# Redrawn tables for the order of a two-MLP kernel, and its last output piece issued by SyncE

## The chip, the cores and the metric

The kernel runs on one core of a Trainium2 chip. The metric is device time in microseconds (us), the median over runs of the same program; the profile is one further execution. The engines are named as in the profile: PE is TensorE (matrix products), DVE is VectorE, ACT is ScalarE, POOL is GpSimd, and SP is SyncE, which here only issues DMAs.

## The reference

Attention over 32 memory slots, then a GELU-like MLP, then an RMS norm and a gated MLP. All arrays are fp32; there are 4 x 576 = 2304 tokens of width 512.

```python
a = exp(phi - max(phi, axis=2))                     # phi: (4, 8, 576, 32)
a = a / (sum(a, axis=2) + 1e-9)
k_m = einsum('bhsm,bhsd->bhmd', a, k)               # q, k, v: (4, 8, 576, 64)
v_m = einsum('bhsm,bhsd->bhmd', a, v)
attn = softmax(q @ k_m.T / sqrt(64))                # over the 32 slots
x = (attn @ v_m).transpose(0, 2, 1, 3).reshape(2304, 512)
h = x @ w_in                                        # 512 -> 2048
x = (h * sigmoid(1.702 * h)) @ w_out                # 2048 -> 512
xn = x / sqrt(mean(x * x, axis=-1) + 1e-6) * rms_g
out = (silu(xn @ w_gate) * (xn @ w_val)) @ w_out2   # 512 -> 1536 -> 512
```

## The kernel before

**Tiles and stages.** The batch is worked in two pairs `pr` of 2 x 576 = 1152 tokens. Attention runs per unit `(b, g)`: batch b, four heads g. `att_k1t` to `att_k5` make the softmax over phi (maxima through a transpose, exponentials, sums) and the small memory keys and values, `att_q1` to `att_q4` the softmax of the queries, which ends in `attnT`. The memory values are multiplied into the first weight (`vm_part`), so that the first MLP is `a_g1` (tokens by vm, then the GELU form, `gf`, split into `gr`) and `a_g2` (by w_out, added into `x2`). `norm_1` to `norm_4` are the RMS norm: squares and their sums, column sums on PE (tile `pnm`), a reciprocal root r by Newton steps on DVE, and its transposes back on PE (`pnr`). `t_a` to `t_d` make the operands of the second MLP, whose gate and value products `s_g3` forms from seven products by the A, S and T blocks of a Strassen-like scheme (tiles `ps_A...`, `ps_S...`), and `s_g4` multiplies by the last weight and adds into `oacc`. `put` writes `oacc` out in pieces of rows; for the last tile of 128 tokens `s_end` works in two halves of 256 columns.

**Precision.** Each fp32 operand is split into a high part that PE multiplies at full rate and the low rest, and each product is three products. For weights this is `w_conv`: two ACT operations on the raw bits, a clamp (`tensor_scalar` with max and min, which the code gives to DVE), two DVE operations on bits, a copy of the high part on ACT and a subtraction of the low part. For weights of the first MLP the clamp works in tile `pad`, for those of the second in tile `cv`; the split weights are written to a cache in DRAM (`cache_a`, `cache_b`, `cache_s`) for the second pair. `w_load` is the DMA of the raw weights (`raw_...`).

**What sets the order.** No instruction is issued where its code stands. The functions add operations to a `Plan`; at the end `Plan.issue` gives all of them to the engines in the order of `Plan.order`. That is a list scheduler with a cost for every operation (`Plan.cost`): on each engine it takes, of the operations that can start soonest, the one with the earliest due time. Due times come from `Plan.dues`: the order of the code on PE, carried back through what depends on what. Two tables bend this. `HASTE` takes a step by its name and arguments (`"att_q4 1 0 0"`) and moves its due time earlier by so many microseconds, and by that what it depends on. `OTHER` names single operations of a step by their place in it; `Plan.add` puts them on DVE if the code gave them to POOL and the other way round:

```python
if k in self.OTHER.get(self.step, ()):
    op.eng = "POOL" if op.eng == "DVE" else "DVE"
```

DMAs all lie on the queue of SP, in planned order, with one exception: in `put`, the smaller row pieces of the last column half are issued by ACT. Where the plan leaves PE idle before a tile, `Plan.fill` puts in products of a constant (`ones_r`). Since `Plan.issue` hands out everything, nearly all rows of the trace have its line (587 before, 611 after).

Of the kernel before, what the change touches and what calls it, by code (L numbers as in the profile page):

```python
# [117 lines left out]
class Plan:  # L118
# [12 lines left out]
    UNIT = {"cache_a": 131072, "cache_b": 65536, "cache_s": 131072}  # L131

    HASTE = {
        "a_g2 0 0 3": 146.2,
        "a_g2 1 1 0": 118.8,
        "att_k1t 0 0": 235.5,
        "att_k2 3 1": 107.7,
        "att_q1 2 1 1": 44.9,
        "att_q3 2 0 0": 108.0,
        "att_q4 1 0 0": 162.7,  # L140
        "att_q4 3 0 0": 115.0,
        "ld_src 0 0 2": 228.6,
        "norm_3 0 2": 113.0,
        "norm_4 0 0 2": 124.5,
        "norm_4 1 1 1": 120.2,
        "s_g4 1 2 1": 212.8,
        "s_g4 1 5 6 False": 27.0,
        "vm_part 0 1 1 0": 174.7,
        "vm_part 1 6 1": 114.4,
        "w_conv c 2 val 0": 124.3,  # L150
        "w_load a 0 1 in 0": 395.9,
    }

    OTHER = {
# [114 lines left out]
    }  # L269

    def __init__(self, nc):
# [18 lines left out]
    def add(self, op):  # L290
        k = self.count[self.step] = self.count.get(self.step, -1) + 1
        op.step = self.step
        if k in self.OTHER.get(self.step, ()):
            op.eng = "POOL" if op.eng == "DVE" else "DVE"
# [296 lines left out]
def kernel(  # L591
# [51 lines left out]
    V, G, A, PE, SP = plan.DVE, plan.POOL, plan.ACT, plan.PE, plan.SP  # L643
# [801 lines left out]
    def put(pr, kk, cols=slice(0, None), last=False):  # L1445
        parts = []
        n0 = kk * P
        while n0 < kk * P + P:
            bb, r = divmod(n0, S)
            r0 = n0 - kk * P  # L1450
            if 2 * pr + bb < N9:
                ln = R9
                to = out_9[2 * pr + bb, r // R9]
            else:
                par, r = divmod(r, HALF)
                cc, p0 = divmod(r, CP)
                ln = min(CP - p0, kk * P + P - n0)
                to = out_v[2 * pr + bb, 2 * cc + par, p0 : p0 + ln]
            parts.append((ln, to[:, cols], oacc[pr][r0 : r0 + ln, kk, cols]))
            n0 += ln  # L1460
        parts.sort(key=lambda x: -x[0])
        for i, (ln, to, x) in enumerate(parts):
            (A if last and i else SP).dma_start(out=to, in_=x)

# [203 lines left out]
    for j, (*key, t) in enumerate(slots):  # L1668
        i = groups.index(tuple(key))
# [39 lines left out]
    for j, (*key, t) in enumerate(slots):  # L1709
        key = tuple(key)  # L1710
        i = groups.index(key)
# [91 lines left out]
```

## Time and profile before

| | us |
|---|---|
| three runs | 837.25, 839.19, 841.02 (median 839.19) |
| profiled execution, its time | 839.06 |
| its span, from first to last instruction | 836.8 |
| PE busy | 819.9 |
| DVE busy | 595.2 |
| ACT busy | 475.7 |
| POOL busy | 246.5 |

The mean granted clock of PE is 0.998 of full speed. Busy times are over the whole span; a wait of PE is read from the view that lists what PE waited for, and from the timelines around it, in which a row shows the start, the duration, the engine, what is written from what, and in brackets the idle time of the engine before it and who ended it.

### The profile page before, as it was taken

The numbers are of one execution on the slowest core, as the hardware profiler recorded it, in microseconds if no ns is written. First come the engines' busy times: TensorE is split into PE (matmuls) and PEld (weight loads), VectorE is DVE, ScalarE is ACT, GpSimd is POOL, SyncE is SP. The second block draws the span as 40 slices with busy tenths as digits, with TensorE's granted clock in tenths as the row PEclk, the third lists the DMA queues.
The fourth block names the chain that finished last, engine by engine and source line by source line (L and its number), as shares of the span: only waits on it lengthen the run. The fifth ranks groups of instructions, "written<-read, shape, count | busy, mean of one in ns | idle before, by whom it ended". The sixth has DMA issues, their size and how long they took to land.

```text
span 836.8 us, 15237 instructions
## 1 busy us (share of the span) xinstructions
PE 819.9 (98%) x5893; PEld 784.1 (94%) x5893; DVE 595.2 (71%) x955; ACT 475.7 (57%) x822; POOL 246.5 (29%) x198
## 2 busy tenths in 40 slices
PE   9899999999999999999999999999999999999997
PEld 7689999999999999999999999999999999999996
DVE  5869599798797778989788688667595334544445
ACT  6897978788788567656666545335352332222221
POOL 3472854475353443345721411001010000000000
PEclk9999999999999999999999999999999999999999
DMA  9995666957967678654666569363356452632504
GB/s 346 297 271 134 225 220 199 298 168 258 281 219 242 223 253 281 231 189 152 180 204 221 176 230 343 129 230 153 112 194 190 157 177 73 205 129 98 176 1 113
DMA packets 76918, 166.92 MB, mean 199 GB/s; under 512 B 7344, under 2 KB 29616, under 8 KB 76848
## 3 DMA queue, kind: packets, MB, share of 16 engines
q1 hardware_dynamic: 76800, 165.93, 60.5%
q8 instruction: 46, 0.75, 0.4%
q14 instruction: 24, 0.20, 0.1%
q10 hardware_dynamic: 48, 0.03, 0.0%
HBM read 106.69 MB, written 59.24 MB: 198 GB/s over the span
## 4 chain that ended last, share of the span: by engine, by line
PE 77%; DMA 6%; ACT 5%; DVE 5%; POOL 3%; issue 2%; SPq 0%; DVEq 0%; POOLq 0%; ACTq 0%
PE pg L587 41%; PE ps_A L587 22%; PE ps_S L587 9%; DMA raw_a_in<-in_moe_w_in_dram 2%; PE pvm L587 2%; DMA cache_b<-cv 2%; DMA stage<-in_v_dram 1%; PE pk L587 1%; PE pq L587 1%; POOL gr L587 1%; POOL pad L587 1%; DVE pad L587 1%; ACT gf L587 1%; DMA kmisc<-in_phi_dram 1%; ACT gr L587 1%
## 5 line engine op out<-in xcount | busy, mean ns | idle before, releaser
L587 PE MATMUL pg<-gr,a_outh 128*128 128x384 f32 (+1 forms) x736 | 193.2, 334 | 2.0 <-DVE x L587 1.3
L587 PEld LDWEIGHTS pg<-gr,a_outh 128*128 128x128 f32 x736 | 132.6, 188 | 2.7 <-DVE x L587 1.6
L587 PE MATMUL pg<-gr,a_outl 128*128 128x384 f32 (+1 forms) x368 | 121.9, 331 | 0.0
L587 ACT COPY c<-ps_A 128x576 f32<-128x576 f32 x72 | 46.1, 640 | 126.1 <-PE ps_A L587 124.9
L587 PE MATMUL pg<-s_o,pp 128*128 128x512 f32 (+1 forms) x438 | 112.2, 387 | 0.0
L587 POOL TENSOR_TENSOR gr<-gf,gr 128x576 fp32r<-128x576 f32 (+2 forms) x62 | 73.1, 1192 | 101.3 <-ACT gr L587 87.6
L587 DVE TENSOR_TENSOR x<-x,pg 128x768 f32<-128x768 f32 (+1 forms) x86 | 79.4, 928 | 26.8 <-PE pg L587 20.0
L587 PEld LDWEIGHTS pg<-s_o,pp 128*128 128x128 f32 x438 | 80.0, 188 | 14.8
L587 DVE TENSOR_TENSOR oacc<-oacc,pg 128x1024 f32<-128x1024 f32 (+2 forms) x55 | 56.5, 1026 | 44.8 <-PE pg L587 44.3
L587 PE MATMUL ps_A<-tba,s_A 128*128 128x288 f32 x576 | 83.4, 295 | 0.0
L587 DVE TENSOR_TENSOR c<-c,ps_S 128x576 f32<-128x576 f32 x48 | 36.2, 754 | 60.8 <-PE ps_S L587 44.7
L587 PEld LDWEIGHTS ps_A<-tba,s_A 128*128 128x128 f32 x576 | 79.0, 188 | 0.4
L587 PEld LDWEIGHTS pg<-gr,a_outl 128*128 128x128 f32 x368 | 69.2, 188 | 0.0
L587 ACT ACTIVATE gf<-pg 128x576 f32<-128x576 f32 x64 | 41.3, 649 | 36.1 <-PE pg L587 29.3
L587 PE MATMUL pg<-s_o,tbd 128*128 128x512 f32 x216 | 60.9, 390 | 0.0
L587 DVE TENSOR_TENSOR c<-c 128x576 f32<-128x576 f32 x44 | 34.0, 772 | 25.0 <-ACT c L587 24.0
L587 ACT CAST gr<-gf 128x576 fp32r<-128x576 f32 (+2 forms) x92 | 45.9, 528 | 2.1 <-PE pg L587 0.5
L587 PEld LDWEIGHTS pg<-s_o,tbd 128*128 128x128 f32 x216 | 39.6, 188 | 7.3
L587 PE MATMUL ps_S<-tbb,s_S 128*128 128x288 f32 x288 | 42.2, 295 | 0.0
L587 PE MATMUL ps_A<-tbc,s_S 128*128 128x288 f32 x288 | 42.1, 295 | 0.0
L587 PE MATMUL ps_S<-tbc,s_S 128*128 128x288 f32 x288 | 42.0, 295 | 0.0
L587 PE MATMUL ps_A<-tbb,s_S 128*128 128x288 f32 x288 | 42.0, 295 | 0.0
(248 smaller groups left out, 1786.1 us busy)
## 6 DMA issues: line engine op xcount, KB each, us to landing
cache_s<-s_S SPq DMA_DIRECT2D x24, 512.0 KB, 4.4
s_S<-cache_s SPq DMA_DIRECT2D x24, 512.0 KB, 4.1
cache_b<-cv SPq DMA_DIRECT2D x36, 256.0 KB, 4.6
raw_a_in<-in_moe_w_in_dram SPq DMA_DIRECT2D x16, 512.0 KB, 5.1
raw_a_out<-in_moe_w_out_dram SPq DMA_DIRECT2D x16, 512.0 KB, 5.8
raw_c_gate<-in_moe_w_gate_dram SPq DMA_DIRECT2D x12, 512.0 KB, 5.2
raw_c_val<-in_moe_w_val_dram SPq DMA_DIRECT2D x12, 512.0 KB, 4.9
raw_c_o<-in_moe_w_out_dram SPq DMA_DIRECT2D x12, 512.0 KB, 4.4
```

The source lines that it names most:

```text
L587: getattr(self.real[op.eng], op.name)(*op.args, **op.kw)
```

## The change

Both tables are replaced. `HASTE` goes from 18 entries to 27, and some of the new ones are negative, so that a step falls due later. `OTHER` is drawn anew; among others, the clamps of `pad` that lie on POOL go from 17 to 6, those of `cv` from 14 to 20. In `put` the condition goes: all pieces are issued by SP. What is computed stays the same, as do the tiles, the loads and the matrix products.

```diff
     HASTE = {
-        "a_g2 0 0 3": 146.2,
...
+        "att_q4 1 0 0": 212.3,
...
+        "s_end 1 5 8": -74.9,
...
     OTHER = {
...
-        "w_conv b 7 vg": (1,),
+        "w_conv b 9 vg": (0, 2, 5),
+        "w_conv c 0 gate 0": (2,),
...
@@ def put
         parts.sort(key=lambda x: -x[0])
         for i, (ln, to, x) in enumerate(parts):
-            (A if last and i else SP).dma_start(out=to, in_=x)
+            SP.dma_start(out=to, in_=x)
```

The first place is the head, where the loads of the first two units and of the first weights share the queue of SP. `stage0_1` holds k, v and q of unit (0, 1), `kmisc2_0` phi of unit (2, 0), `raw_a_0_1_in_1` half of a raw weight, and `cache_a` receives the split weights of the group before. Before, on SP:

```order
L587 DMA raw_a_0_0_out_1_160<-in_moe_w_out_dram 128x1024
L587 DMA raw_a_0_1_in_0_172<-in_moe_w_in_dram 128x2x512
L587 DMA stage0_1_118<-in_q_dram 128x2x576
L587 DMA cache_a_98<-a_0_0_inh_122 128x1024
L587 DMA raw_a_0_1_in_1_174<-in_moe_w_in_dram 128x2x512
L587 DMA kmisc2_0_239<-in_phi_dram 96x2x192 x2
L587 DMA cache_a_98<-a_0_0_inl_123 128x1024
```

After, on SP:

```order
L611 DMA stage0_1_118<-in_v_dram 128x2x576
L611 DMA raw_a_0_1_in_0_172<-in_moe_w_in_dram 128x2x512
L611 DMA stage0_1_118<-in_q_dram 128x2x576
L611 DMA kmisc2_0_239<-in_phi_dram 96x2x192
L611 DMA raw_a_0_1_in_1_174<-in_moe_w_in_dram 128x2x512
L611 DMA kmisc2_0_239<-in_phi_dram 96x2x192
L611 DMA cache_a_98<-a_0_0_inh_122 128x1024
L611 DMA cache_a_98<-a_0_0_inl_123 128x1024
```

Both writes to `cache_a` now stand behind the raw weight `raw_a_0_1_in_1` and behind the two loads of phi; the last half of the weight before, `raw_a_0_0_out_1`, has moved ahead of the load of v. Earlier in the queue, q of unit (0, 0) has moved ahead of phi of that unit.

On ACT, a little later in the head: `pad` and `raw_a_...` are the first two operations of `w_conv`, `stage0_1` (384 and 192 wide) the exponentials of the query softmax of unit (0, 1), `vm0_0h` the high part of the first `vm_part`, `attnT0` the result of `att_q4`. Before:

```order
L587 ACTIVATE pad_121<-raw_a_0_1_out_1_179 128x512
L587 ACTIVATE raw_a_0_1_out_1_179<-raw_a_0_1_out_1_179,ulp_97 128x512
L587 ACTIVATE stage0_1_118<-stage0_1_118 128x384
L587 CAST vm0_0h_161<-pvm_164 64x256 x2
L587 ACTIVATE pad_121<-raw_a_0_2_in_0_234 128x512
L587 ACTIVATE stage0_1_118<-stage0_1_118 128x192
L587 CAST attnT0_139<-pq4_140 128x384
```

After:

```order
L611 ACTIVATE stage0_1_118<-stage0_1_118 128x384
L611 CAST vm0_0h_161<-pvm_163 64x256 x2
L611 ACTIVATE stage0_1_118<-stage0_1_118 128x192
L611 CAST vm0_0h_161<-pvm_164 64x256 x2
L611 CAST attnT0_139<-pq4_140 128x384
L611 ACTIVATE pad_121<-raw_a_0_2_in_0_234 128x512
L611 ACTIVATE raw_a_0_2_in_0_234<-raw_a_0_2_in_0_234,ulp_97 128x512
```

The exponential of 192 columns and the copies of `vm0_0h` have gone ahead of the conversion of `raw_a_0_2_in_0`, and that conversion behind the first copy into `attnT0`. Earlier in ACT's order, both operations of the conversion of `raw_a_0_1_in_1` now stand ahead of the copy of `pk5` (the memory keys of unit (0, 0)); before, only the first did.

On POOL, in the same stretch, clamps of `pad` stood between the small operations of the softmax; they are on DVE now. Near the addition into `x2_0` from `pg2_306` (at 112 us in the trace of before), two subtractions of `a_0_3_outl` that POOL had are on DVE, ahead of that addition.

The second place is the norm of the second pair's first tile, on PE. `pnm` are the column sums, `pnr` the transposes of r, and the products between them belong to the gated MLP of the first pair. Before:

```order
L587 MATMUL pnm_798<-ones_f_91,sm_797 128x1 x3
L587 MATMUL ps_A12_812<-tba0_661,s0_1_A11_788 128x288 x12
L587 MATMUL ps_A11_784<-tbd0_779,s0_0_A22_753 128x288 x12
L587 MATMUL ps_A11_811<-tbb0_674,s0_1_S1_789 128x288 x12
L587 MATMUL pnr_805<-ident_90,r_799 128x128 x3
```

After:

```order
L611 MATMUL pnm_798<-ones_f_91,sm_797 128x1 x3
L611 MATMUL ps_S1_800<-tbc0_690,s0_0_S3_754 128x288 x12
L611 MATMUL ps_A11_784<-tbd0_779,s0_0_A22_753 128x288 x12
L611 MATMUL ps_A11_811<-tba0_661,s0_1_A11_788 128x288 x12
L611 MATMUL ps_A12_812<-tba0_661,s0_1_A11_788 128x288 x12
L611 MATMUL pnr_805<-ident_90,r_799 128x128 x3
```

Four products of twelve matmuls stand between column sums and transposes in place of three. The column sums of another norm (`pnm_566`, at 276 us in the trace of before) have moved later in PE's order by some 44 us of products.

The third place is the end of SP's order, the output pieces of the last tile. Before, the last piece of 32 rows was issued by ACT:

```order
L587 DMA out_0_dram<-oacc1_1065 64x512 x2
L587 DMA out_0_dram<-oacc1_1065 96x256
L587 DMA out_0_dram<-oacc1_1065 32x256
L587 DMA out_0_dram<-oacc1_1065 96x256
L1798 UNCONDITIONAL_BRANCH
```

After:

```order
L611 DMA out_0_dram<-oacc1_1065 64x512 x2
L611 DMA out_0_dram<-oacc1_1065 96x256
L611 DMA out_0_dram<-oacc1_1065 32x256
L611 DMA out_0_dram<-oacc1_1065 96x256
L611 DMA out_0_dram<-oacc1_1065 32x256
L1822 UNCONDITIONAL_BRANCH
```

The piece now stands last on SP, and ACT issues no DMA any more.

## Rows read from the trace of the kernel before

**Rows 1.** The page, busy us with share of the span and number of instructions.

```profile
PE 819.9 (98%) x5893; PEld 784.1 (94%) x5893; DVE 595.2 (71%) x955; ACT 475.7 (57%) x822; POOL 246.5 (29%) x198
```

**Rows 2.** Timelines of PE, ACT and SP at the tail: start us, us, engine, operation.

```profile
831.29 1.00 PE L587 MATMUL pg<-s_o,pp 128*128 128x256 f32 x7
...
832.78 0.43 ACTq L587 DMA_DIRECT2D out_dram<-oacc  x1
...
833.92 0.42 SPq L587 DMA_DIRECT2D out_dram<-oacc  x1
```

**Rows 3.** What PE waited for, whole span: us in total, times, longest us.

```profile
PE pq L587 <- ACT stage L587: 1.4, 1, 1.4
PE pnr L587 <- DVE r L587: 1.4, 1, 1.4
PE pg L587 <- DVE x L587: 1.3, 1, 1.3
...
PE pq L587 <- DVE stage L587: 1.2, 2, 0.7
PE pk L587 <- DVE mx L587: 1.1, 2, 0.6
PE pq L587 <- POOL stage L587: 0.9, 2, 0.6
...
PE pnm L587 <- ACT gf L587: 0.6, 1, 0.6
```

**Rows 4.** Timeline of all engines, 424 to 434 us.

```profile
427.77 1.75 PE L587 MATMUL ps_A<-tbb,s_S 128*128 128x288 f32 x12
...
428.70 1.44 POOL L587 TENSOR_TENSOR c<-c 128x576 f32<-128x576 f32 x1 [4.95 <-ACT c L587]
428.78 1.38 DVE L587 SCALAR_TENSOR_TENSOR r<-r 128x3 f32<-128x3 f32 x1
...
430.90 0.51 PE L587 MATMUL pnr<-ident,r 128*128 128x128 f32 x3 [1.37 <-DVE r L587]
```

**Rows 5.** Windows: us, busy of PE, PEld, DVE, ACT, POOL, clock, DMA share, GB/s.

```profile
8.00:10.00 2.00, 2.00 (x10) 1.74 (x10) 1.53 (x5) 1.97 (x4) 0.00 (x0) 1.00 1.05 386
340.00:400.00 60.00, 59.87 (x389) 59.54 (x387) 56.78 (x73) 36.49 (x61) 24.30 (x17) 1.00 0.59 201
440.00:832.00 392.00, 392.00 (x2503) 366.30 (x2502) 231.43 (x353) 146.22 (x250) 28.51 (x23) 1.00 0.48 164
```

**Rows 6.** Timeline of ACT in the head.

```profile
24.77 0.66 ACT L587 ACTIVATE pad<-raw_a_in 128x512 f32<-128x512 f32 x1 [1.33 <-DMA raw_a_in<-in_moe_w_in_dram]
...
25.74 0.80 ACT L587 ACTIVATE raw_a_in<-raw_a_in,ulp 128x512 uint32<-128x512 uint16 x1
...
35.45 0.67 ACT L587 ACTIVATE pad<-raw_a_in 128x512 f32<-128x512 f32 x1 [0.61 <-DMA raw_a_in<-in_moe_w_in_dram]
36.02 0.35 ACT L587 ACTIVATE stage<-stage 128x192 f32<-128x192 f32 x1
```

**Rows 7.** Timeline of POOL in the head.

```profile
33.10 1.92 POOL L587 TENSOR_SCALAR pad<-pad 128x512 f32<-128x512 f32 x1 [0.43 <-ACT pad L587]
35.09 0.25 POOL L587 TENSOR_SCALAR stage<-stage 128x6 f32<-128x6 f32 x1
```

**Rows 8.** Timeline of all engines, 106 to 118 us.

```profile
108.89 2.37 DVE L587 SCALAR_TENSOR_TENSOR pad<-raw_a_out,pad 128x512 uint32<-128x512 uint32 x1
...
110.10 1.92 POOL L587 TENSOR_SCALAR pad<-pad 128x512 f32<-128x512 f32 x1
...
111.18 0.68 DVE L587 SCALAR_TENSOR_TENSOR pad<-pad,raw_a_in 128x512 uint32<-128x512 uint32 x1
...
113.65 0.45 PE L587 MATMUL pg<-gr,a_outh 128*128 128x384 f32 x1 [1.35 <-DVE x L587]
```

**Rows 9.** Clamps by line and form: count, busy us, mean ns, idle us before.

```profile
L587 POOL TENSOR_SCALAR pad<-pad 128x512 f32<-128x512 f32 x17 | 35.6, 2095 | 19.4 <-ACT pad L587 19.3
L587 DVE TENSOR_SCALAR pad<-pad 128x512 f32<-128x512 f32 x15 | 7.2, 493 | 3.8 <-ACT pad L587 3.6
```

More of the change, by code (lines that the diff above doesn't have):

```diff
@@ L133 @@
     HASTE = {
-        "a_g2 0 0 3": 146.2,
[L135 to L149, printed above, removed]
@@ L150 @@
-        "w_conv c 2 val 0": 124.3,
-        "w_load a 0 1 in 0": 395.9,
+        "a_g1 0 0 1": 159.8,
+        "att_k3 2 0": 106.1,
+        "att_k3s 3 1": 130.1,
+        "att_k5 2 1": 88.9,
+        "att_q1 2 1 1": 83.8,
+        "att_q3s 1 1 0": 174.7,
+        "att_q4 1 0 0": 212.3,
+        "att_q4 2 1 0": 83.8,
+        "ld_src 0 0 2": 389.2,
+        "norm_1 1 2": 132.5,
+        "norm_3 0 1": 100.0,
+        "norm_4 0 0 0": 121.1,
+        "norm_4 0 2 0": 121.1,
+        "s_end 1 5 8": -74.9,
@@ L152 @@
+        "s_g3 1 9 2": 80.1,
+        "s_g4 1 0 0": 95.9,
+        "s_g4 1 4 4": 60.3,
+        "s_g4 1 5 3 False": 21.4,
+        "s_g4 1 5 5 False": -141.8,
+        "s_g4 1 5 7 False": -40.0,
+        "t_d 0 0": 194.3,
+        "vm_part 0 1 1 0": 219.3,
+        "vm_part 1 6 1": 117.0,
+        "w_conv a 0 2 in 1": 83.7,
+        "w_load a 0 1 in 0": 427.4,
+        "w_load c 5 gate 1": 131.2,
+        "w_load s 1 vg": 184.9,
     }
     OTHER = {
+        "a_g1 0 0 1": (14,),
         "a_g1 0 0 2": (14,),
[4 rows of a table removed]
+        "a_g1 0 1 3": (14,),
@@ L160 @@
+        "a_g1 0 2 0": (14,),
         "a_g1 0 3 1": (14,),
         "a_g1 0 3 3": (14,),
[3 rows of a table removed]
+        "a_g1 0 4 0": (14,),
+        "a_g1 0 4 1": (16,),
+        "a_g1 0 4 2": (14,),
+        "a_g1 0 4 3": (14,),
+        "a_g1 0 5 1": (16,),
+        "a_g1 0 5 3": (14,),
         "a_g1 0 6 0": (14,),
+        "a_g1 0 6 1": (16,),
+        "a_g1 0 6 3": (14,),
         "a_g1 1 0 0": (14,),
[16 rows of a table removed]
+        "a_g1 1 0 3": (14,),
+        "a_g1 1 2 1": (14, 16),
+        "a_g1 1 2 3": (14,),
+        "a_g1 1 3 2": (14, 16),
@@ L183 @@
+        "a_g1 1 3 3": (14,),
+        "a_g1 1 4 0": (14,),
+        "a_g1 1 4 1": (16,),
+        "a_g1 1 5 1": (14, 16),
+        "a_g1 1 5 2": (14, 16),
+        "a_g1 1 5 3": (14,),
+        "a_g1 1 6 1": (14,),
+        "a_g1 1 6 2": (14, 16),
+        "a_g1 1 6 3": (14,),
+        "a_g1 1 7 1": (14,),
+        "a_g1 1 7 2": (14,),
+        "a_g1 1 7 3": (14,),
         "att_k3 1 0": (2,),
@@ L185 @@
         "att_k3 2 1": (2,),
[6 rows of a table removed]
+        "att_k3s 0 0": (0,),
+        "att_k3s 0 1": (0,),
+        "att_k3s 1 0": (0, 1),
+        "att_k3s 1 1": (0,),
+        "att_k3s 2 0": (2,),
+        "att_k3s 2 1": (0,),
+        "att_k3s 3 0": (1,),
+        "att_k3s 3 1": (2,),
         "att_k4 0 0": (23,),
[1 row of a table removed]
         "att_k4 1 1": (27,),
[9 rows of a table removed]
+        "att_k4 3 0": (27,),
+        "att_q3s 0 0 0": (1,),
+        "att_q3s 0 1 0": (1, 3),
+        "att_q3s 0 1 1": (3,),
+        "att_q3s 1 0 0": (1,),
+        "att_q3s 1 1 0": (1,),
+        "att_q3s 2 0 0": (1,),
+        "att_q3s 2 1 0": (3,),
+        "att_q3s 3 0 0": (1,),
+        "att_q3s 3 1 0": (3,),
+        "norm_1 0 0": (2, 3),
+        "norm_1 0 2": (3,),
+        "norm_1 1 0": (2, 3),
         "norm_1 1 1": (2, 3),
[3 rows of a table removed]
+        "norm_1 1 2": (2,),
+        "norm_2 0 1": (12,),
+        "norm_2 1 1": (9,),
         "norm_2 1 2": (12,),
[15 rows of a table removed]
+        "s_g3 0 0 2": (26, 28, 29),
+        "s_g3 0 1 2": (29, 33),
+        "s_g3 0 11 2": (28, 30),
+        "s_g3 0 2 2": (26,),
+        "s_g3 0 7 2": (26, 33),
+        "s_g3 1 3 2": (31,),
+        "s_g3 1 6 2": (26, 28),
+        "s_g3 1 7 2": (26,),
+        "t_a 0 0": (3,),
+        "t_b 0 0": (1, 3),
+        "t_b 0 1": (0, 1, 3),
+        "t_c 0 0": (1, 4),
+        "t_c 0 1": (1, 2, 7),
+        "t_c 1 0": (5,),
+        "t_c 1 1": (2, 5),
+        "t_d 0 1": (1,),
         "w_conv a 0 0 in 0": (6,),
@@ L227 @@
         "w_conv a 0 1 in 0": (6,),
[4 rows of a table removed]
+        "w_conv a 0 1 in 1": (6,),
+        "w_conv a 0 2 in 1": (6,),
+        "w_conv a 0 2 out 0": (2,),
         "w_conv a 0 3 in 1": (2,),
[20 rows of a table removed]
+        "w_conv a 0 3 out 0": (6,),
+        "w_conv a 0 3 out 1": (6,),
+        "w_conv a 0 4 in 0": (2,),
+        "w_conv a 0 4 in 1": (2, 6),
+        "w_conv a 0 4 out 0": (6,),
+        "w_conv a 0 4 out 1": (6,),
+        "w_conv a 0 5 out 1": (6,),
+        "w_conv a 0 6 in 1": (2,),
+        "w_conv a 0 7 in 0": (2,),
+        "w_conv a 0 7 in 1": (6,),
+        "w_conv a 0 7 out 0": (6,),
+        "w_conv b 0 vg": (2, 5),
+        "w_conv b 1 vg": (11,),
+        "w_conv b 10 o2": (1,),
+        "w_conv b 10 vg": (2,),
+        "w_conv b 11 vg": (1, 2),
+        "w_conv b 2 vg": (11, 14),
+        "w_conv b 3 vg": (0, 1, 2, 3, 5, 11, 14),
+        "w_conv b 4 vg": (1, 5, 8),
+        "w_conv b 5 vg": (1,),
         "w_conv b 6 vg": (11,),
[1 row of a table removed]
+        "w_conv b 9 vg": (0, 2, 5),
+        "w_conv c 0 gate 0": (2,),
+        "w_conv c 0 gate 1": (2,),
         "w_conv c 0 val 1": (2,),
[2 rows of a table removed]
         "w_conv c 1 o2 0": (2,),
+        "w_conv c 2 gate 0": (2,),
         "w_conv c 2 gate 1": (2,),
[1 row of a table removed]
+        "w_conv c 2 o2 0": (2,),
         "w_conv c 2 val 1": (2,),
@@ L263 @@
         "w_conv c 3 o2 1": (2,),
+        "w_conv c 3 val 0": (2,),
+        "w_conv c 4 gate 0": (2,),
         "w_conv c 4 gate 1": (2,),
[1 row of a table removed]
+        "w_conv c 4 o2 0": (2,),
+        "w_conv c 4 val 0": (2,),
         "w_conv c 5 gate 0": (2,),
[1 row of a table removed]
+        "w_conv c 5 gate 1": (2,),
+        "w_conv c 5 o2 0": (2,),
         "w_conv c 5 val 0": (2,),
+        "w_conv c 5 val 1": (2,),
     }
```

83 rows, old and new, of the table OTHER are left out of this document.

## Prediction

> **What bounds the kernel now.** I read the profile from the outside in. The busy table says that TensorE (PE) is busy for 819.9 of 836.8 us [rows 1]: the span is PE's own work with 16.9 us of gaps, and no other engine is near a bound over the whole. The change leaves every matrix product and every load as it is and draws only their order and the engine of some small operations anew. So it can take from these 16.9 us and add to them, and nothing else. Part of the gaps is the tail, in which the last results leave the chip. The tail is read from the queues: ScalarE issues its piece at 832.78 and SyncE its last one at 833.92, and the span ends at 836.8 [rows 2]; the last matmuls start at 831.29 and last 1.00 us, so the tail is 836.8 − 832.3 = 4.5 us. There remain 16.9 − 4.5 = 12.4 us, the start and the waits inside the program. The table of what PE waited for lists them; seven of its fourteen rows carry the argument, from 1.4 us down to 0.6 [rows 3]. The last of them by time is at 430.90 [rows 4]; from 440 to 832 us PE is busy without a gap [rows 5], so there the change has nothing to win, only to lose.
>
> The timelines around the largest waits say who is late, and it is never an engine's total. In the head ScalarE stands 1.33 us before a conversion whose raw weights have not landed, and the copy that PE wants is queued behind that conversion [rows 6]. A little later an exponential at 36.02 stands behind another such conversion, which idled 0.61 us for its DMA [rows 6], and a small GpSimd (POOL) operation at 35.09 behind a clamp of 1.92 us [rows 7]. Near 112 us VectorE (DVE) is late with an addition: one of its operations took 2.37 us beside a POOL clamp of 1.92, where the same operation took 0.68 next to it [rows 8]. Near 430 one step of the reciprocal root r took 1.38 us for three numbers per partition, beside a POOL addition of 1.44 [rows 4].
>
> **The change part by part.** The sum is made against the profiled run, 839.06 us with a span of 836.8; the median of the three runs lies 0.13 us higher, which I neglect.
>
> *Head, loads.* The 512 KB of raw weights now come ahead of a 512 KB write to the cache in the queue. In the first stretch of rows 5 the transfers run at 386 GB/s, in the two later ones at 201 and 164; at 386, 512 KB take 1.36 us, about the 1.33 that ScalarE idled. In exchange one more conversion of 0.80 us [rows 6] stands ahead of the copy. I take 1.33 − 0.80 = 0.55 us off PE's 1.4 [rows 3]; bounds are the whole 1.4, and nothing, if the load comes no sooner. The queries q now stand before phi; 576 KB at 386 GB/s is 1.5 us by which the softmax over phi starts later. PE spends those first 16 us partly on dummy products, which absorb it: I take +0.3, from 0 to +1.5.
>
> *Head, softmax of the first two units.* The exponential no longer stands behind the conversion that waits for its DMA, and no POOL clamp of 1.92 us stands ahead of the small POOL operations. The waits of PE for this chain are 1.2 (DVE) and 0.9 (POOL) [rows 3], 2.1 in all. A released chain usually meets its next link, here DVE, which has taken over the clamps at 0.49 us each [rows 9]; I take −1.0, from 0 to −2.1. The transposed maxima (1.1 us in two waits [rows 3]) now have a group of products before one of the two: −0.5, from 0 to −1.1. The head comes to −0.55 + 0.3 − 1.0 − 0.5 = −1.75.
>
> *Clamps.* Of the 17 clamps of pads on POOL (2.1 us each, 1.92 undisturbed) eleven go to DVE, where one takes 0.49 [rows 8, 9]: 5.4 us more of DVE, 23 less of POOL. At 112 us this removes the neighbour that held DVE for 2.37 − 0.68 = 1.69 us, more than PE's whole wait of 1.35 [rows 8]. But DVE also receives two weight subtractions and some small operations ahead of the addition. I take −0.7, from −1.35 to 0.
>
> What rows 4 and 8 show is that a DVE operation beside a POOL one lasts until about the end of the POOL one. The Trainium skill, "SBUF — State Buffer", section "Who interferes with whom", says that these two engines take one pair of ports as an exclusive lock for a whole instruction, and that the later one blocks fully; it counts DVE's fast single-input operations among the holders. That speaks against part of this edit: a clamp on DVE would still hold the pair, so that POOL stands instead, though for the 0.49 us of rows 9 and not 1.92. By that rule the gain at 112 would be at most 1.35 − 0.49 = 0.86 instead of 1.35, and the sum's ends would close by half a microsecond.
>
> *Norms.* The column sums for one norm near 276 us, for which PE waited 0.6 [rows 3], stand much later in PE's order, past other products: −0.57, with 0 as the other end. Before the transposes of r near 430, PE now has four products of twelve matmuls instead of three; one takes 1.75 us by the product that starts at 427.77, against a wait of 1.37 [rows 4]. I take −1.2, from 0 to −1.37, since r itself may be held again.
>
> *Tail.* The two 32-row pieces leave on SyncE only. The last one of ScalarE took 0.43 us to issue at 832.78, beside SyncE's own; now it stands behind SyncE's issue of 833.92, which lasts 0.42 [rows 2]. Its issue therefore ends near 834.8, and nothing lies beside it: +0.45 us, from 0.3 to 0.6. This is the one term that I hold for nearly certain.
>
> *New waits.* An order drawn anew for the whole program will meet operations that last longer than was planned for, as this one does. In the redrawn stretch from 100 to 440 us the three waits of the old order that I take out come to 1.4 + 1.3 + 0.6 = 3.3 us [rows 3]. New ones may be none, or as many again. I take +1.2, about a third, from 0 to +3.3; this is a choice, not a reading.
>
> Sum: −1.75 − 0.7 − 0.57 − 1.2 + 0.45 + 1.2 = −2.57 us, or 839.06 − 2.57 = **836.5 us**.
>
> **Rivals.** *All waits found above go and none comes:* −1.4 − 2.1 − 1.1 − 1.35 − 0.57 − 1.37 + 0.45 = −7.44, or 831.6 us. For it: each of these waits has its cause named in a row, and the order moves that cause. Against: only the first link of each chain is seen, and three of the sites are in the head, where transfers run at 386 GB/s [rows 5], so that a load moved forward moves another one back.
>
> *Waits only change places:* the new order loses as much as the old one elsewhere, and only the tail's 0.45 is left, 839.5 us. For it: PE has only some 12 us of waits in 836.8, each below 1.5, of the size by which a single operation differs from its plan. The change would then not do what it says, as far as time goes.
>
> *Slower, by POOL in the gated MLP's weight stage:* POOL's clamps of the second MLP's weights go from 14 to 20. From 340 to 400 us DVE is busy for 56.78 of 60 us, so 3.2 us are its slack, and PE is 59.87 busy beside it [rows 5]. Each clamp can hold a DVE operation for 1.69 us as in rows 8; six give 10.1, less 3.2 of slack leaves 6.9 us for PE. It decides as soon as more than two of the six strike (2 × 1.69 = 3.4 > 3.2). Time: 839.06 − 1.75 + 0.45 + 6.9 = 844.7. For it: DVE is fullest just there. Against: six clamps leave DVE for POOL in exchange, and PE has work of other groups between the additions. The exclusive lock of the Trainium skill, "SBUF — State Buffer", section "Who interferes with whom", would make each of the six strike whenever DVE runs an operation with two on-chip inputs; rows 4 and 8 agree on the form, and no row here shows how often.
>
> **How the numbers follow.** Forecast 836.5 us with a chance of 0.44 (its own range 834.5 to 838.5); all waits gone, 0.20; waits change places, 0.27; POOL in the weight stage, 0.09. The range from 831.8 to 841.0 holds the forecast, the waits that move, and most of the case in which all go; it leaves out POOL's case and the lower half of the best one, about 2 in 10. A measurement of this kernel tells about 0.5% from no change, 4.2 us, so "faster" begins below 835.0 and "slower" above 843.4. Faster: nearly all of the second case and a fifth of the first, 0.29. Slower: POOL's case, 0.08. The same: 0.63.
>
> **What would show it.** In the changed kernel the list of what PE waited for should lack the 1.4 of r, the wait of the column sums and that of the copy in the head; the timeline near 35 us should show no POOL clamp among the small operations. In the tail a fifth DMA on SyncE should start near 834.3 relative to the old end, and the end of the last matmul be followed by 4.9 to 5.1 us in place of 4.5. If PE's busy time is not 819.9 within 1 us, the premise that the work is the same is wrong, or the clock was. If DVE is above 58 of 60 us in a stretch where PE now waits, the last rival was right. The forecast is wrong if the waits of PE sum to less than 7 us or to more than 13.

## The result and the profile after

The changed kernel takes 831.16 us (median of 6 runs, 830.17 to 832.02) beside 839.61 us (6 runs, 837.25 to 841.53) for the kernel before: a ratio of 0.990, interval 0.988 to 0.992. That is 8.4 us less. In a later comparison it took 831.18 against 836.78: 0.9931, interval 0.9913 to 0.9948, or 5.6 us. The changed kernel takes the same time in both; the kernel before does not, and its single runs spread over 834.6 to 841.5 us. The forecast was 836.5 with a range that ended at 831.8, so the gain is real, of the sign forecast, and 2.2 to 3.3 times the 2.57 us of the sum.

The profiled execution of the changed kernel took 831.05 us with a span of 828.8. The first row is the page's table of busy times, the answer to [rows 1]:

```profile
PE 816.8 (99%) x5893; PEld 782.2 (94%) x5893; DVE 593.1 (72%) x951; ACT 466.3 (56%) x810; POOL 237.7 (29%) x202
```

PE's busy time is 3.1 us below the 819.9 of before, though the products are the same. The span is 8.0 us shorter (836.8 to 828.8): 5.1 us less of waits, 3.1 us less of busy time, 0.2 us more of tail.

What PE waited for in the changed kernel (us in total, times, longest us), all nine rows, where the kernel before had fourteen [rows 3]:

```profile
PE pk L611 <- DVE kmisc L611: 2.2, 1, 2.2
PE pq L611 <- DVE stage L611: 1.6, 2, 1.2
PE pk L611 <- DVE maskeo L1613: 1.3, 1, 1.3
PE pq L611 <- ACT stage L611: 0.6, 1, 0.6
PE pq L611 <- DVE vm_0l L611: 0.4, 2, 0.2
PE pvm L611 <- DVE vll L611: 0.4, 1, 0.4
PE pk L611 <- DVE mx L611: 0.3, 1, 0.3
PE pk L611 <- ACT stage L611: 0.2, 1, 0.2
PE pg L611 <- DVE vm_0l L611: 0.2, 1, 0.2
```

They sum to 7.2 us, where the fourteen of before sum to 12.3, and the last wait of the changed kernel is at 71 us. The waits for x, r, gr and gf have no row any more. The tail, as in [rows 2], from the timelines of PE and SP (start us, us, engine, operation):

```profile
822.79 1.24 PE L611 MATMUL pg<-s_o,pp 128*128 128x256 f32 x9
...
823.36 3.16 SPq L611 DMA_DIRECT2D out_dram<-oacc  x6
```

PE ends at 824.03, the span at 828.8: 4.75 us, against 4.54 before.

**Where the time went.** Since both kernels do the same products, their traces can be laid beside each other by the work done: I gave each product the median distance of its kind to the next one in the trace of before, left the dummy products out, and read when each kernel had done so many of the 788 us of work. Differences to the profiled execution of before, in us (minus is earlier):

```
work done   before at   after    h_new56  h_old56  e_sites  e_clock
   5          22.5      +1.07     +0.71    +0.45    +1.51    -0.32
  10          31.2      -1.57     -1.24    +0.06    -0.88    -1.11
  15          41.5      -1.70     -2.37    +1.77    +1.85    -0.21
  60          92.9      -2.67     -2.59    +1.32    +1.70    -0.20
 260         301.7      -5.65     -3.45    -1.66    +0.98    -0.88
 350         392.0      -5.80     -2.95    -1.82    +2.30    -0.52
 400         444.5      -8.36     -3.89    -2.68    -0.01    -1.66
 780         823.9      -8.26     -3.88    -2.57    -0.00    -1.66
```

(The last four columns belong to experiments below.) The changed kernel loses 1.1 us in its first 22 us, gains 3.7 from there to 93 us, and gains 5.6 more between 93 and 444 us, at the places of the late waits of before. After 444 us nothing happens in either. (The row of work 10 falls in the half-clock stretch of before and depends on the exact weights by up to 1.5 us; the others do not, within 0.15.)

The late gain is in PE's waits: the five of before between 93 and 444 us (at 113, 221, 276, 400 and 430 us) are 4.4 us of gaps, and at each of them the next product starts 0.16 us later than the gap alone would make it, since products overlap. The early gain mostly is not: up to 93 us the gaps fell from 7.9 to 7.2 us, and the other 1.9 us are busy time. Most of that is the stretch from 28 to 32 us, where the granted clock of before was 0.59 (its row stands with the dummy products below). In the changed kernel:

```profile
28.00:32.00 4.00, 3.83 (x69) 3.40 (x68) 2.82 (x10) 2.83 (x7) 0.37 (x2) 1.00 1.02 398
```

ScalarE loads its function tables 15 times in the changed kernel and 21 times before, at 1.28 us each: 7.7 of the 9.4 us by which its busy time fell. No run here takes this part of the change alone.

### The profile page after: what moved, and what is told of

It reads as the page before. It is cut to its first block, busy times and chain, and to the rows that moved or that the text cites. A ratio compares the mean times of both kernels' runs of the same rounds, so it can differ in the third digit from the quotient of the medians.

```text
span 828.8 us, 15239 instructions
## 1 busy us (share of the span) xinstructions
PE 816.8 (99%) x5893; PEld 782.2 (94%) x5893; DVE 593.1 (72%) x951; ACT 466.3 (56%) x810; POOL 237.7 (29%) x202
## 4 chain that ended last, share of the span: by engine, by line
PE 94%; DMA 2%; DVE 2%; ACT 1%; issue 1%; SPq 0%; DVEq 0%
PE pg L611 54%; PE ps_A L611 23%; PE ps_S L611 9%; PE pvm L611 3%; PE pq L611 2%; PE pk L611 2%; DMA raw_a_out<-in_moe_w_out_dram 1%; DMA kmisc<-in_phi_dram 1%; DVE stage L611 1%; ACT stage L611 0%; PE pnm L611 0%; SPq L611 0%; ACT pad L611 0%; DVE vm_0l L611 0%; DVE pad L611 0%
## 5 line engine op out<-in xcount | busy, mean ns | idle before, releaser
L611 POOL TENSOR_TENSOR gr<-gf,gr 128x192 fp32r<-128x192 f32 (+2 forms) x55 | 58.1, 1069 | 87.7 <-ACT gr L611 73.6
L611 DVE TENSOR_TENSOR c<-c 128x576 f32<-128x576 f32 x41 | 31.8, 777 | 22.1 <-ACT c L611 20.7
L611 POOL TENSOR_SCALAR cv<-cv 128x512 f32<-128x512 f32 x20 | 40.5, 2031 | 9.2 <-DMA raw_b_o<-cache_b 4.1
L611 PE MATMUL ps_A<-tbd,s_A 128*128 128x288 f32 x288 | 42.1, 295 | 0.0
```

The source lines that it names most:

```text
L611: getattr(self.real[op.eng], op.name)(*op.args, **op.kw)
```

## The experiments

Ratios stand to runs of the kernel before on the same chip in the same session, which took 836.5 to 837.2 us there (medians of 17 to 30 runs).

**The halves of the new order.** For these two kernels both orders were planned, and a cut was made at 56 us of planned time: what the one order had begun by then came first, the rest followed in the other order.

```diff
+        head = [x for x in self.drawn(self.HEAD_OLD) if x[0] < self.CUT]
+        rest = [x for x in self.drawn(not self.HEAD_OLD) if x[1] not in done ...]
+        return [(op, eng) for _, op, eng in head + rest]
```

New head, old rest:

> Order and engines of the changed kernel for everything planned in the first 56 us, the order and engines of the kernel before for the rest; all output pieces by SyncE. Lined up by the matrix work done, the changed kernel leads by 2.2 us at 60 us of its time. Theory (the gain is a sum of separate waits, each gone at its own place): 839.6 - 2.2 + 0.2 for the tail = 837.6 us, and PE's waits after 100 us as in the kernel before (1.35 at 112, 0.5 at 221, 0.6 at 276, 0.7 at 400, 1.4 at 430). Rival A (the early stage decides, the later waits go with it): 831 to 833. Rival B (the early lead is given back at the next late load): 839.5 or more.

Measured: 834.98 us, 0.9977 (0.9958 to 0.9997). The late waits of before are back in its list of what PE waited for, those for x and r among them:

```profile
PE pk L775 <- DVE kmisc L775: 1.6, 1, 1.6
PE pg L775 <- DVE x L775: 1.3, 1, 1.3
...
PE pnr L775 <- DVE r L775: 1.0, 1, 1.0
```

Old head, new rest:

> The mirror of the run before: order and engines of the kernel before for the first 56 us, those of the changed kernel for the rest. Theory of separate waits: 831.2 + 2.2 = 833.4 us, with PE's clock at half for some 3 us after 28 us and no wait above 0.5 us after 100 us. Rival A (the early stage decides): 838 to 840. Rival B (an early lead is given back): 831.

Measured: 834.59 us, 0.9972 (0.9957 to 0.9986). Together the halves give 0.9949, and the whole change in the later comparison 0.9931; the intervals overlap. So within these intervals the gain is a sum over the two halves, as the theory of separate waits has it, with no sign that one half needs the other. The table of leads shows the same: the head of h_new56 brings 2.4 us by work 15; its rest brings 1.5 more, as much as e_clock, which is the old order too, gains there by chance. h_old56 starts 1.8 late and gains 4.3 from there on. The absolute times that I expected, 837.6 and 833.4, were built on a kernel before at 839.6.

**Three operations moved in the old order.** The swap is made on the finished order, so that no other instruction moves. The first and the third are neighbours of a late operation, the second is itself late. Of the three moves only the second is one of the change's, whose table leaves the clamp (`w_conv a 0 4 in 1`) and the addition (`s_g3 0 0 2`) on POOL.

```diff
+        for key, eng in [
+            (("w_conv a 0 4 in 1", 2), "DVE"), (("a_g1 1 7 1", 14), "DVE"), (("s_g3 0 0 2", 26), "DVE"),
+        ]:
+            seq[at(key)][1] = eng
```

> The kernel before in its own order; three single operations go from POOL to DVE at their place and nothing else: the clamp of pad that ran beside the held DVE operation at 110 us, the subtraction gr that took 2.98 us on POOL at 397.5 us between DVE operations, and the addition c at 428.7 us beside the step of r that took 1.38. Theory (DVE and POOL hold each other, and these three waits come from it): the waits of 1.35, 0.66 and 1.37 us go, 839.6 - 3.4 = 836.2 us. Rival (they come from a full DVE, or meet a next late operation): each operation that DVE gets is added to its queue, the waits stay or shrink by under a third, 838.5 to 840.

Measured: 836.54 us, 1.0004 (0.9989 to 1.0020): no gain. Its list of what PE waited for says which of the three went:

```profile
PE pg L773 <- DVE x L773: 1.1, 1, 1.1
...
PE pg L773 <- DVE vm_6l L773: 0.7, 1, 0.7
```

The waits at 400 and 430 us are gone (neither gr nor r has a row), which the table of leads puts at 2.3 us between work 350 and 400. The wait for x near 112 us stayed at 1.1 of 1.35: the clamp was a small part of what made the addition late. The VectorE operation that took 2.37 us in the kernel before still takes 1.79, beside a POOL subtraction. The timeline of the kernel before shows that subtraction too, and a longer hold ahead of it, a VectorE subtraction of a form that takes 0.55 us undisturbed:

```profile
104.49 3.76 DVE L587 TENSOR_TENSOR gr<-gf,gr 128x384 fp32r<-128x384 f32 x1
...
109.12 1.01 POOL L587 TENSOR_TENSOR gr<-gf,gr 128x384 fp32r<-128x384 f32 x1
```

And a wait for vm_6l has come at 362 us, ahead of the two edits that worked, so not through them; it is 0 in the profile of before, and the old order shows a gap of 0.3 and 0.2 us next to it in the traces of h_new56 and e_clock. So two of the three causes were right, but the theory's 3.4 us are not in the time: the measured bound is a gain of at most 0.9 us. Where the rest went is not settled. Part of it was never there: the kernel before has its 0.7 us gap at 400 us in the profile that the prediction used, and one of 0.1 or none in h_new56 and e_clock, which run the same order there.

**Dummy products in the idle stretch.**

```diff
+        i = at(("att_q3 0 0 0", 0))
+        seq[i:i] = [[Fill((ap,), dict(lhsT=self.ones, rhs=rhs, start=True, stop=True)), "PE"] for _ in range(6)]
```

> The kernel before in its own order, with six dummy products of 512 columns (1.28 us together) put on PE ahead of the products that wait 1.4 us for ScalarE's copy at 24.3 us. Nothing else changes. Theory (the half clock from 28 to 32 us follows PE's idle stretch from 24 to 28 us, and costs 4 x (1 - 0.59) = 1.6 us): the clock stays at full speed there and the time is 839.6 - 1.6 = 838.0 us. Rival (the clock falls for another reason, or the time it costs lies beside other waits): the clock falls all the same or the time stays at 839.6.

Measured: 837.58 us, 1.0012 (0.9991 to 1.0034). The stretches of the kernel before and of this one (us, busy us of PE, PEld, DVE, ACT, POOL with counts, granted clock, DMA share, GB/s), first before:

```profile
24.00:28.00 4.00, 2.11 (x33) 1.54 (x31) 3.04 (x8) 2.99 (x7) 2.13 (x2) 0.98 1.05 379
28.00:32.00 4.00, 4.00 (x55) 3.49 (x54) 2.85 (x10) 3.45 (x10) 0.43 (x2) 0.59 0.95 315
```

then with the dummy products:

```profile
24.00:28.00 4.00, 3.07 (x37) 2.22 (x36) 2.68 (x8) 2.96 (x7) 2.12 (x2) 1.00 1.05 390
28.00:32.00 4.00, 3.28 (x64) 2.65 (x62) 3.20 (x10) 3.77 (x13) 0.82 (x2) 1.00 0.92 311
```

The first half of the theory holds: with PE busy for 3.07 instead of 2.11 of 4 us, the clock stays at its upper level, 2.4 GHz, where it had been at 1.2 for most of the second stretch. The second half falls: PE does the same work faster and then waits, 3.28 of 4 us busy instead of 4.00. A lead of 1.1 us at work 10 is one of 0.2 at work 15, and the time does not move. By work 60 PE's busy time without the dummy products is 2.3 us lower than before, and the gain is 0.2: in the head, what PE saves comes back as idle time or lies under the dummy products. Its waits there are for the softmax of the queries (1.8 us for VectorE's `stage` in place of 1.2), so that this chain probably binds.

**The changed kernel again, and three edits to it.**

> The changed kernel unchanged, once more beside the kernel before. The two halves of the new order brought 0.9977 and 0.9972 of the time of before when each was put together with the other half of the old order. Theory (separate waits that add up): 0.9977 x 0.9972 = 0.995, on a chip where the kernel before takes 836.5 about 832.3 us. Rival (the halves need each other, or the first comparison holds as it stands): 0.990, 828 us. In either case the spread of its runs shows whether it is steadier than the kernel before, whose runs lay between 834.6 and 841.1.

Measured: 831.18 us, 0.9931, between the theory's 0.995 and the rival's 0.990. Its interval (0.9913 to 0.9948) excludes 0.990 and just excludes 0.9949, which is itself a product of two measurements; the theory is the nearer one, but not clearly met. Six runs lie within 829.6 to 833.5, seventeen of the kernel before beside them within 835.5 to 840.0.

Next, two operations of the head were moved within their engine's queue. The reason is in the changed kernel's timeline at 12 us, VectorE and POOL, the largest wait in its list:

```profile
12.12 1.33 POOL L611 TENSOR_TENSOR a_outl<-pad,a_outh 128x512 fp32r<-128x512 f32 x1 [9.37 <-ACT a_outh L611]
...
12.25 1.28 DVE L611 TENSOR_TENSOR kmisc<-kmisc,y 128x64 f32<-128x64 f32 x1
```

The same maximum over 64 columns takes 0.22 us elsewhere; here it ends as the POOL subtraction does.

```diff
+        for step, ks, anchor, n in [("w_conv a 0 0 out 0", [4], ("att_k1t 0 0", 3), 1), ("att_q3 0 0 0", [14], ("w_conv a 0 1 out 0", 0), 0)]:
+            rows = [seq.pop(at((step, k))) for k in ks]
+            i = at(anchor) + n
+            seq[i:i] = rows
```

> The changed kernel with two operations put elsewhere in its own order: on VectorE, the last step of the conversion of the first w_out half goes behind the four maxima of phi of unit (0, 0), and on ScalarE the exponential of 384 columns of unit (0, 0) goes ahead of the conversion of raw_a_0_1_out_0, which idled 1.09 us for its DMA. Theory (the two waits of PE in the head, 2.2 us for kmisc and 1.2 for the softmax of the queries, are set by the row ahead of the late operation): the first falls by about 1 us, the second by 1.2; 2.2 us less than the changed kernel run beside it. Rival (the lead is given back at the next load or by a full VectorE and ScalarE before 41 us): within 0.5 us of the changed kernel.

Measured: 830.92 us, 0.9930 (0.9915 to 0.9945), beside 831.18 for the changed kernel: no difference that can be told. In its trace both edits did what they should: the maximum takes 0.22 us, and the wait for kmisc falls from 2.2 to 1.1 (it is 1.5 to 3.6 in the other executions with this head); the exponential starts at 28.50 in place of 30.28 us, and the wait for VectorE's `stage` falls from 1.6 to 0.9. What PE waited for, the first rows:

```profile
PE ps_A L773 <- ACT c L773: 1.9, 1, 1.9
...
PE pk L773 <- DVE kmisc L773: 1.1, 2, 0.6
PE pq L773 <- ACT stage L773: 1.0, 1, 1.0
PE pq L773 <- DVE stage L773: 0.9, 1, 0.9
```

By work 15 this execution leads the changed kernel by 1.16 us, and keeps it up to 420 us; there it loses 3.7 us. It begins with a wait of ScalarE for the cache write of a tile that the copy needs:

```profile
419.96 0.65 ACT L773 ACTIVATE c<-ps_A 128x576 f32<-128x576 f32 x1 [4.03 <-DMA cache_b<-cv]
```

PE stands 1.9 us for it, and then its clock falls. The stretches of this execution:

```profile
422.00:424.00 2.00, 1.72 (x11) 1.72 (x12) 2.00 (x4) 1.83 (x4) 0.24 (x2) 0.89 0.26 109
424.00:428.00 4.00, 4.00 (x22) 4.00 (x21) 4.00 (x7) 0.64 (x1) 1.32 (x1) 0.63 0.20 83
```

From 424 to 428 us PE is busy throughout and does 22 products; the changed kernel, at 1.00, does 33 there. The two stretches lose 2 x 0.11 + 4 x 0.37 = 1.7 us by the clock, and no later wait gives them back. In the profile of the changed kernel ScalarE stands there too, without harm to PE:

```profile
418.67 0.65 ACT L611 ACTIVATE c<-ps_A 128x576 f32<-128x576 f32 x1 [2.12 <-DMA cache_b<-cv]
```

Both writes were issued within 0.2 us of each other, at 414.7 and 414.9, and landed at 418.6 and 419.9; the load ahead of it landed 1.3 us late in the one execution. h_old56, which runs the same order there, has the wait as well, with 1.3 us, and two of the runs below have it with 0.2 and 0.4; the two executions of the unaltered changed kernel have none. So a new wait of this kind does exist in the new order, in some executions. Whether the lead in the head would show in the time without it is not settled by these runs.

Now the clamps. Thirteen are concerned: two further ones went the other way, so that POOL's count of clamps fell by eleven.

```diff
+        for key in ['w_conv a 0 1 in 1', 'w_conv a 0 1 out 1', 'w_conv a 0 2 in 0', ..., 'w_conv a 0 7 out 1']:
+            seq[at((key, 2))][1] = "POOL"
```

> The changed kernel in its own order; only the thirteen clamps of pad that POOL had before and VectorE has now are given back to POOL, each at its place. Theory (a clamp on POOL holds up VectorE, or a conversion behind it, so that moving the clamps carries a good part of the gain): 2 us or more above the changed kernel, with waits for x or for the softmax of the queries back. Rival (the clamps on POOL are hidden, the gain is in the order): within 0.7 us of the changed kernel.

Measured: 837.62 us, 1.0004 (0.9991 to 1.0016): the whole gain is gone, 6.4 us above the changed kernel beside it. By work done, its execution loses 5.9 us against the changed kernel's, 3.0 of them near 56 us. The timeline from 52 to 57 us (start us, us, engine, operation, idle before and its releaser) shows this largest piece:

```profile
52.34 1.91 POOL L771 TENSOR_SCALAR pad<-pad 128x512 f32<-128x512 f32 x1
...
54.28 1.89 DVE L771 SCALAR_TENSOR_TENSOR pad<-pad,raw_a_in 128x512 uint32<-128x512 uint32 x1 [1.65 <-POOL pad L771]
56.10 0.22 DVE L771 TENSOR_SCALAR rv<-maskeo,rv 128x3 f32<-128x3 f32 x1
...
56.35 0.31 ACT L771 ACTIVATE kz<-pk,rv 128x64 f32<-128x64 f32 x1 [1.77 <-DVE rv L771]
...
56.72 0.44 PE L771 MATMUL pk<-ident,kz 128*128 128x128 f32 x2 [1.11 <-ACT kz L771]
```

The next DVE operation in the queue waits for the clamp, then runs beside a POOL subtraction and takes 1.89 us for 0.68; the small rv, on which ScalarE's kz and PE hang, is queued behind both. Afterwards PE's clock is at half, as the window of 58 to 60 us of the same kernel shows in its third column from the end (0.50):

```profile
58.00:60.00 2.00, 2.00 (x10) 2.00 (x10) 0.00 (x0) 1.54 (x6) 2.00 (x2) 0.50 0.92 340
```

In the changed kernel the same four steps:

```profile
52.21 0.42 DVE L611 TENSOR_SCALAR pad<-pad 128x512 f32<-128x512 f32 x1
...
52.66 0.69 DVE L611 SCALAR_TENSOR_TENSOR pad<-pad,raw_a_in 128x512 uint32<-128x512 uint32 x1
...
53.27 0.22 DVE L611 TENSOR_SCALAR rv<-maskeo,rv 128x3 f32<-128x3 f32 x1
...
54.32 0.33 ACT L611 ACTIVATE kz<-pk,rv 128x64 f32<-128x64 f32 x1
```

rv is 2.8 us earlier, and PE never waits for kz. So this clamp costs by its own length (1.91 us for 0.42), since VectorE stands for its result. In the head, where two of the thirteen lie, giving them back costs next to nothing: by work 15 this execution leads before by 1.6 us, the changed kernel by 1.7. That any other thirteen operations moved out of place would cost as much has not been tried.

**One clamp, and the clock behind it.**

```diff
+        seq[at(("w_conv a 0 2 in 0", 2))][1] = "POOL"
```

> The changed kernel with a single clamp given back to POOL, that of raw_a_0_2_in_0 at 52 us. With all thirteen given back, VectorE stood 1.65 us for this one, the reciprocal for kz behind it came late, PE waited 1.1 us at 56 and its clock was at half from 58 to 61 us. Theory (this clamp carries half of the loss, and the half clock costs time here since PE is the bound from then on): 1.1 + 0.5 x 3.5 = 2.9 us above the changed kernel, 834. Rival (without the others VectorE has room): within 0.5 us of the changed kernel.

Measured: 833.27 us, 0.9959 (0.9943 to 0.9974). That is 2.1 us above the changed kernel of the other comparison (0.9931, 0.9913 to 0.9948), and the two intervals just touch; in the trace PE loses 1.7 us between work 25 and 30, where e_pads lost 3.0. The half clock did not come in this execution (1.00 in every window from 50 to 64 us), so its price is not in these 1.7; in e_pads it was.

> As the run with a single clamp given back, with five dummy products of 512 columns (1.07 us) on PE in the place where it waits for kz. Theory (the half clock follows PE's idle stretch and costs time where no other engine binds): the clock stays at full speed, 1.7 us less than with the single clamp alone. Rival (as in the head, the clock's time lies beside other waits): the same time as with the single clamp alone.

Its edit adds five dummy products ahead of `("att_k5 1 0", 0)`, as in the earlier run with six. Measured: 832.33 us, 0.9943 (0.9923 to 0.9962), which overlaps the run before, and the trace shows the same 1.7 us. Since the clock had not fallen without the dummy products, this pair does not tell the theory from its rival.

**The same clamps in the old order.** The edit is that of e_pads with "DVE" for "POOL", on the order of the kernel before.

> The kernel before in its own order; only the thirteen clamps of pad that the changed kernel has on VectorE and the kernel before on POOL go to VectorE, each at its place. Given back to POOL in the changed kernel's order they cost 6.4 us. Theory A (a clamp on POOL costs wherever it stands): the same gain the other way, 831 to 833 us where the kernel before takes 836.6. Theory B (the new order is drawn around clamps on VectorE, so that only clamps beside a late operation count): the wait at 112 us goes, the rest stays or VectorE gets later by some of 13 x 0.49 us, 835 to 838 us.

Measured: 837.78 us, 1.0009 (0.9992 to 1.0026): theory B. In its trace the wait for x at 112 us is gone, worth 1.3 us, but others stand, and one is new:

```profile
PE pnr L771 <- DVE r L771: 1.4, 1, 1.4
...
PE pnm L771 <- POOL sm L771: 0.9, 1, 0.9
```

**One table alone.**

> The kernel before with the new choice between VectorE and POOL and with all pieces issued by SyncE, but with the old due times; the order is planned anew from these. Theory (the two tables fit only each other, each table alone meets as many waits as the old pair): between 836 and 841 us where the kernel before takes 836.5 to 839.6. Rival (the choice of engines carries the gain): at most 833 us.

> The kernel before with the new due times and all pieces issued by SyncE, but with the old choice between VectorE and POOL; the order is planned anew from these. The mirror run, new choice with old due times, took 857 us. Theory (the two tables fit only each other): clearly above the kernel before, 845 us or more. Rival (the due times carry the gain and only the choice of engines is fragile): at most 836 us.

Measured: 857.12 us (four runs; 1.0248, interval 1.0226 to 1.0270) with the new choice of engines and the old due times, 853.28 us (two runs; 1.0196, 1.0166 to 1.0227) the other way round. The first expectation missed on both readings, 836 to 841 and at most 833; the second came out as its theory had it. Each table alone costs 16 to 20 us; the losses lie between 41 and 494 us of the time of before. Most of them were planned: the plan itself put in 121 and 95 dummy products in place of 59, and PE is busy for 835.3 and 830.2 us. So these two runs compare plans with more idle time in them. They show that neither table gives the gain alone, and not which places carry it.

## Why the prediction missed

Two steps of the sum failed. It said that the change can take from the 16.9 us of gaps "and nothing else", and it put a made-up loss of 1.2 us against the gains. In the profiles the gaps gave 4.9 us (16.9 to 12.0, the tail included) and PE's busy time gave 3.1, a term that the sum had at nothing. The prediction's own sign for this, busy time off 819.9 by more than 1 us, has come: the work is the same, but the half-clock stretch of before is gone, 1.6 us, and so is the 0.16 us of overlap at each late wait. By e_clock the first brings no time by itself: in the head PE's busy time and its waits pass into each other, and a list of waits is no measure of what can be won there. Its sign on the waits, a sum below 7 or above 13 us, has not come (7.2). That nothing happens after 440 us was right.

The likeliest case was not the one that came. The second, in which all waits found go and none comes, gave 831.6 against 831.16 measured. That is partly luck: it took 4.6 us of waits out of the head, where 0.7 of gaps went, and 3.3 out of the late stretch, which gained 5.6.

- **New waits, +1.2: wrong, and the largest single miss among the waits.** The two profiles of the changed kernel have no wait in PE's list after 72 us. The term was a choice and not a reading. e_head_act and h_old56 show that such waits exist in some executions (1.9 and 1.3 us).
- **112 us, −0.7 of 1.35; 276, −0.57; 430, −1.2.** All three waits went whole. The places were right, the cause at 112 us was not: the clamp named there stays on POOL in the changed kernel, and its move in e_sites left 1.1 of the wait. What took the wait away is open; in e_clamps, which moves other clamps, it went too. Two further waits, at 221 (0.5) and 400 us (0.7), were in the trace and in no term; both are gone. Between 93 and 444 us the sum had −2.5 + 1.2 = −1.3, the profile has −5.6: 4.4 of gaps, 0.8 of overlap at them, and 0.4 that I can't place.
- **What the clamps do: mis-sized, and for the wrong reason.** I booked them at one place, 112 us, and by the neighbour that they hold. Given back within the new order they cost 6.4 us, the whole gain; moved within the old order they bring nothing. They are worth something only in an order drawn for them: not a cost of their own, but a condition of the new order. The account edit by edit, against the old order, could not see that.
- **Head, −1.75: near in sum, wrong in parts.** By work 60 the profile has −2.67, of which 0.7 are gaps. The load of q that was to cost 0.3 cost 1.07: phi landed at 9.91 in place of 8.24 us, 1.7 later, where 1.5 had been the upper bound, and VectorE's maximum beside a POOL subtraction took 1.06 more; of both together 1.07 was left at 22 us. The copy at 24 us gained 0.8 in place of 0.55, the maxima 0.8 in place of 0.5. The waits for the softmax of the queries fell from 2.1 to 1.6 us with 0.4 new ones for vm_0l behind them, in place of −1.0, and the POOL clamps named as one cause are worth 0.15 there (e_pads). Still, the last products of that softmax start at 37.08 in place of 38.68 us. Rows of VectorE for the start of the softmax over phi, before and after:

```profile
8.72 0.36 DVE L587 TENSOR_TENSOR y<-kmisc 128x192 f32<-128x192 f32 x1 [0.47 <-DMA kmisc<-in_phi_dram]
...
10.43 0.36 DVE L611 TENSOR_TENSOR y<-kmisc 128x192 f32<-128x192 f32 x1
```

- **Tail, +0.45: sign right, half the size.** 4.75 − 4.54 = 0.2 us; all ten profiles with all pieces on SyncE have 4.7 to 4.8, the four with the piece on ScalarE 4.5.
- **POOL in the weight stage, +6.9: did not come.** PE is busy for all of 300 to 440 us.
- **The rule on the shared ports.** The reading that it was laid on, that a VectorE operation lasts until the end of its POOL neighbour, holds in rows 4 and not in rows 8: the operation of 2.37 us ended at 111.26, the clamp at 112.02, and the next VectorE operation took its usual 0.68 beside that clamp. In the fourteen traces 195 VectorE operations of this form (128x512, on bits) ran beside a POOL clamp alone and none took more than 1.12 us, where undisturbed they take 0.62 to 0.70; beside POOL's two-input operations they took up to 2.41. So a clamp holds VectorE by some 0.4 us at most, and the price of 1.69, in the rival on the weight stage too, was read off the wrong neighbour. Rows of e_pads agree with the Trainium skill, "SBUF — State Buffer", section "Who interferes with whom", in that VectorE's 0.68 us two-input operation took 1.89 beside a POOL subtraction.
- **The baseline.** The profile used had more gaps than the kernel before usually has: 0.5 us at 221 and 0.7 at 400, of which h_new56 and e_clock, in the same order, show 0.1 or nothing. In the later comparison the gain is 5.6 us, not 8.4.

## What to carry to other kernels

Where one engine is busy for 98% of the span, list every wait of that engine, take each one from its own chain, and do not put a made-up loss against the gains: either a row names where a new wait comes from, or its term is zero with a bound. Look at the clock in the engine's busy time too, which is not fixed by the work alone. Name a neighbour that holds an operation only after checking when it starts and ends, and that the change moves it. A table that orders a whole program is not a sum of edits; put parts of it into the old program and the time says little about it, whereas taking one part out of the new program shows that the order needs it. And measure the kernel before often: here its runs spread over more than 6 us, more than most of the terms.

## What the runs showed of the hardware

A fall of the granted clock cost its time where PE was the bound and nothing where it was not. In e_clock the fall between 28 and 32 us was taken away and the time stayed, for PE then waited. In e_head_act the fall after 422 us, with PE busy throughout, cost 1.7 us for good. The runs are mixed in the same way: of 30 runs of the kernel before on one chip, seven had a mean clock below 0.995 and took 836.8 us on average, twelve had 0.998 or more and took 836.7; of 17 on another chip, four below 0.995 took 839.4 and seven with 0.998 or more 836.5.

VectorE and POOL hold each other in both directions. In the kernel before a POOL subtraction of 128x192, 0.6 us elsewhere (106.65 us in its timeline), took five times as long beside four two-input operations of VectorE in a row (397.33 to 400.01 us):

```profile
397.49 2.98 POOL L587 TENSOR_TENSOR gr<-gf,gr 128x192 fp32r<-128x192 f32 x1 [5.12 <-ACT gr L587]
```
